# Second MLP product of a fused attention and MLP kernel by Strassen's scheme

## The chip, the cores and the metric

The kernel runs on one core of a Trainium2 chip. The metric is the device time of one execution in microseconds (us). Before the change it is 687.11 us, the median of three runs (686.88 to 687.49).

## What is computed

Softcapped attention over 4 batches, 12 heads, 448 positions and 64 columns a head, then an MLP with a squared ReLU on the 1792 tokens of 768 columns. The MLP's weights arrive in float64.

```python
scores = cap * np.tanh(scale * np.matmul(q, k.transpose(0, 1, 3, 2)) / cap)
attn = np.exp(scores - np.max(scores, axis=-1, keepdims=True))
attn = attn / (np.sum(attn, axis=-1, keepdims=True) + 1e-09)
x = np.matmul(attn, v)          # then heads side by side: 1792 x 768
h = np.maximum(x @ w_in, 0.0)   # w_in: 768 x 2048
out = h * h @ w_out             # w_out: 2048 x 768, out: 1792 x 768
```

## The kernel before

Three stretches follow each other. **Attention** runs over 24 pairs of heads. The **first product** makes `g = relu(x @ w_in)^2`, one block of 128 hidden columns (f = 0 to 15) and one batch at a time, 18 matmuls each (line 290), and writes g to DRAM (`g_dram`, line 296). The **second product** multiplies g with `w_out`. This change is about the second product.

Every float32 operand of a matmul is split in two float32r parts, a rounded one and the rest (`gh` and `gl` for g, `ohi` and `olo` for the weights), and a product takes three matmuls: high by high, high by low, low by high (lines 672 to 674). g is split by `split_g`: a DMA on SP's queue brings 1 MB of g from DRAM (line 621), ScalarE copies it to `gh` with rounding (line 624), VectorE subtracts (`gl`, line 625). The weights come by `load_wout`: a DMA of half a block of 128 rows (128x384 float64, line 258), then `decode_f64` (lines 44 to 56), which makes the two float32r parts from the 64-bit words by two ScalarE and seven VectorE instructions of 128x384. For four halves of `w_in` the last addition (line 56) is on GpSimd.

16 blocks f of weights by 14 tiles of 128 tokens by two halves `o` of 384 columns by three parts are 1344 matmuls of 384 columns. Nine of the 16 weight blocks (`NOUT1`) are decoded during the first product, seven (`wo2`) in the first part of the second. Four token tiles run side by side until all weights are there, each with its own PSUM banks; the other ten go one after the other, `gh` and `gl` in three buffers (pool `g`). `put` copies a finished 128x384 block out of PSUM on ScalarE (line 679) and writes it with two DMAs, one on SP's and one on ScalarE's queue (line 683).

Up to the end of attention the order of instructions is written by hand. Behind it a scheduler sets it by its own cost estimates, with `issue_after` holding the decoding of `w_out` behind the first product's results. Every engine, and each queue that issues DMAs, works through its list strictly in order.

Of the kernel before, what the change touches and what calls it, by code (L numbers as in the profile page):

```python
# [169 lines left out]
def tile_softcap_attention_mlp(ctx, tc, q, k, v, cap, w_in, w_out, out):  # L170
# [463 lines left out]
    marks = {NEARLY - 2: (last["square"], last["g"]), NEARLY - 1: (last["square"], last["g"])}
# [22 lines left out]

    with ExitStack() as mctx:
        op = mctx.enter_context(tc.tile_pool(name="o", bufs=2))
        gp = mctx.enter_context(tc.tile_pool(name="g", bufs=3))  # L660
        wo2 = mctx.enter_context(tc.tile_pool(name="wo2", bufs=NF - NOUT1))
        ps_o = mctx.enter_context(tc.tile_pool(name="ps_o", bufs=NSIDE - 1, space=PSUM))
        outs = {}

        def mlp2(tt, o, f):
            if f == 0 and o == 0:
                outs[tt] = (ps_o if tt % NSIDE else ps_f).tile([P, 2, 512], F32, tag="o", name="po")
            po = outs[tt]
            gh, gl = gs[tt, f]
            hi, lo = wout[f]  # L670
            os_ = slice(o * HO, (o + 1) * HO)
            nc.tensor.matmul(out=po[:, o, :HO], lhsT=gh, rhs=hi[:, os_], start=(f == 0), stop=False)  # L672
            nc.tensor.matmul(out=po[:, o, :HO], lhsT=gh, rhs=lo[:, os_], start=False, stop=False)  # L673
            nc.tensor.matmul(out=po[:, o, :HO], lhsT=gl, rhs=hi[:, os_], start=False, stop=(f == NF - 1))  # L674

        def put(tt, o):
            po = outs[tt]
# [7 lines left out]
        for f in range(FG, NF, FG):  # L685
            split_g(gp, slice(f, f + FG), side)
        for f in range(nout, NF):
            load_wout(f, wo2, scr2)
# [49 lines left out]
```

## Time and profile before

| | before |
|---|---|
| median of three runs | 687.11 us (686.88 to 687.49) |
| the profiled execution: span from first to last instruction | 684.9 us; what lies around the span is 2.2 us of the median |
| TensorE busy with matmuls | 669.2 us, 98% of the span |
| VectorE, ScalarE, GpSimd busy | 390.8, 309.7 and 113.8 us |
| second product on TensorE | 443.95 to 678.58 us of the span |

The profile is of one execution. Matmuls are pipelined, so the duration of one (335 ns for 384 columns) is longer than the distance of two starts. PE is TensorE, PEld its weight loads, DVE VectorE, ACT ScalarE, POOL GpSimd, SP the engine that issues most DMAs.

### The profile page before, as it was taken

Reading aid. Unit: us, or ns where it says so; the run is one execution under the profiler, and the core shown is the slowest. Engines: PE = TensorE matmul, PEld = TensorE weight load, DVE = VectorE, ACT = ScalarE, POOL = GpSimd, SP = SyncE. Lnnn points to the kernel's source line nnn. Section 1 sums busy time; section 2 is a strip of 40 time slices with the busy share of each in tenths; the row PEclk is TensorE's granted clock in tenths of the full one; section 3 lists DMA queues with packets and bytes.
Section 4 is the critical chain, followed back from the end, with each engine's and each line's share of the span. In section 5 each row is a group of like instructions: output and inputs, shape, how many; then the busy total and the mean of one; then the engine's idle time right before and its main releaser. Section 6 shows DMA issues by size and latency. Waiting matters only on the chain.

```text
span 684.9 us, 10575 instructions
## 1 busy us (share of the span) xinstructions
PE 669.2 (98%) x3882; PEld 549.9 (80%) x3882; DVE 390.8 (57%) x799; ACT 309.7 (45%) x454; POOL 113.8 (17%) x201
## 2 busy tenths in 40 slices
PE   6999999999999999999999999999999999999995
PEld 5444555555554799999999999999999999999995
DVE  4577878878776545599999997169840111111100
ACT  5898989878888231344334433143341111111000
POOL 8655545555420010000000000000000000000000
PEclk9999999999999999999999999999999999999999
DMA  7345446545441331475546446157544332333101
GB/s 177 86 111 137 118 120 146 133 120 121 113 113 42 118 134 68 137 226 165 182 152 201 159 157 196 66 164 211 155 108 120 85 85 84 85 85 85 34 25 28
DMA packets 95932, 83.11 MB, mean 121 GB/s; under 512 B 39072, under 2 KB 86688, under 8 KB 95872
## 3 DMA queue, kind: packets, MB, share of 16 engines
q1 hardware_dynamic: 86768, 68.50, 34.6%
q0 software_dynamic: 6112, 10.91, 6.5%
q10 hardware_dynamic: 2992, 2.93, 1.3%
q8 instruction: 33, 0.54, 0.3%
q14 instruction: 27, 0.22, 0.1%
HBM read 61.87 MB, written 20.27 MB: 120 GB/s over the span
## 4 chain that ended last, share of the span: by engine, by line
PE 96%; DMA 1%; ACT 1%; DVE 0%; SPq 0%; issue 0%; ACTq 0%; DVEq 0%
PE hps L290 34%; PE po L672 11%; PE po L673 11%; PE po L674 11%; PE sc L363 9%; PE pa L403 8%; PE pb L395 3%; PE pa L387 3%; PE tp L339 2%; PE sc L345 2%; DMA wraw<-in_moe_w_in_dram 1%; DMA kn<-in_k_dram 1%; ACT p L370 0%; SPq L321 0%; SPq L320 0%
## 5 line engine op out<-in xcount | busy, mean ns | idle before, releaser
L290 PE MATMUL hps<-xs,kqh 128*128 128x448 f32 x576 | 161.9, 362 | 0.0
L672 PE MATMUL po<-ohi,gh 128*128 128x384 f32 x448 | 149.7, 335 | 0.6 <-ACT osb L679 0.6
L673 PE MATMUL po<-olo,gh 128*128 128x384 f32 x448 | 150.0, 335 | 0.0
L674 PE MATMUL po<-ohi,gl 128*128 128x384 f32 x448 | 148.4, 335 | 0.0
L290 PEld LDWEIGHTS hps<-xs,kqh 128*128 128x128 f32 x576 | 107.9, 187 | 9.2
L290 PE MATMUL hps<-xs,kql 128*128 128x448 f32 x288 | 105.8, 367 | 0.0
L625 DVE TENSOR_TENSOR gl<-graw,gh 128x2048 fp32r<-128x2048 f32 x14 | 32.1, 2291 | 123.4 <-ACT gh L624 114.0
L370 ACT ACTIVATE p<-sc,qks 128x896 f32<-128x896 f32 x96 | 82.4, 911 | 12.7 <-PE sc L363 12.7
L375 ACT ACTIVATE p<-p,cap_sb 128x896 f32<-128x896 f32 x96 | 85.7, 948 | 0.0
L672 PEld LDWEIGHTS po<-ohi,gh 128*128 128x128 f32 x448 | 84.0, 188 | 0.9 <-ACT osb L679 0.9
L673 PEld LDWEIGHTS po<-olo,gh 128*128 128x128 f32 x448 | 84.1, 188 | 0.0
L674 PEld LDWEIGHTS po<-ohi,gl 128*128 128x128 f32 x448 | 83.9, 188 | 0.0
L294 ACT ACTIVATE r<-hps 128x448 f32<-128x448 f32 x64 | 34.7, 542 | 82.1 <-PE hps L290 78.2
L624 ACT CAST gh<-graw 128x2048 fp32r<-128x2048 f32 x14 | 26.7, 1910 | 90.6 <-PE po L673 80.8
L295 DVE TENSOR_TENSOR r<-hps,r 128x448 f32<-128x448 f32 x64 | 39.6, 620 | 47.0 <-ACT r L294 46.8
L403 PE MATMUL pa<-p,vn 128*64 128x448 f32 x288 | 59.4, 548 | 0.0
L44 ACT ACTIVATE mag<-wraw 128x384 f32<-128x384 f32 x64 | 34.7, 553 | 49.5 <-DVE olo L56 30.5
L290 PEld LDWEIGHTS hps<-xs,kql 128*128 128x128 f32 x288 | 54.1, 188 | 3.5
L290 PE MATMUL hps<-xs,whi 128*128 128x448 f32 x192 | 54.1, 363 | 0.0
L403 PEld LDWEIGHTS pa<-p,vn 128*64 128x64 f32 x288 | 18.5, 136 | 39.9 <-issue 39.9
L363 PE MATMUL sc<-kqh 64*128 64x448 f32 (+1 forms) x168 | 42.6, 441 | 5.1 <-ACT p L370 4.5
L379 DVE TENSOR_TENSOR add<-p 128x896 f32<-128x896 f32 x24 | 26.2, 1091 | 34.2 <-PE pb L395 34.2
(79 smaller groups left out, 892.0 us busy)
## 6 DMA issues: line engine op xcount, KB each, us to landing
g_dram<-r SPq DMA_DIRECT2D x64, 224.0 KB
graw<-g_dram SPq DMA_DIRECT2D x14, 1024.0 KB
wraw<-in_moe_w_in_dram SPq DMA_DIRECT2D x32, 384.0 KB
wraw<-in_moe_w_out_dram SPq DMA_DIRECT2D x32, 384.0 KB
rb<-rd SPq DMA_DIRECT2D x48, 112.0 KB
vn<-in_v_dram POOLq DMA_DIRECT2D x48, 64.0 KB, 2.7
qn<-in_q_dram SPq DMA_DIRECT2D x44, 64.0 KB
kn<-in_k_dram POOLq DMA_DIRECT2D x44, 64.0 KB, 3.1
```

Of the source, the lines that this page charges most:

```text
L44: yield nc.scalar.activation(out=magf, in_=high.bitcast(F32), func=ACTF.Abs, scale=2.0 ** 16)
L290: nc.tensor.matmul(out=ps, lhsT=w[:, c * P:(c + 1) * P], rhs=x[b, c], start=(n == 0), stop=(n == 3 * KDM - 1))
L294: nc.scalar.activation(out=r, in_=ps, func=ACTF.Relu)
L295: last["square"] = nc.vector.tensor_mul(out=r, in0=ps, in1=r)
L363: nc.tensor.matmul(out=sc[:, h, :S], lhsT=kx[r, t * P:(t + 1) * P], rhs=qx[r, 4 * P:], start=(s == 0), stop=(s == 2))
L370: nc.scalar.activation(out=p, in_=probs[n, u][:, :c, :S], func=ACTF.Tanh, scale=qks)
L375: nc.scalar.activation(out=p, in_=p, func=ACTF.Exp, scale=cap_sb)
L403: nc.tensor.matmul(out=pvs[n, 0][r], lhsT=vn[n % NKV][:, h, u - 1], rhs=p[:, h], start=False, stop=(u == NU - 1))
L625: nc.vector.tensor_sub(out=gl, in0=graw, in1=gh.bitcast(F32))
L672: nc.tensor.matmul(out=po[:, o, :HO], lhsT=gh, rhs=hi[:, os_], start=(f == 0), stop=False)
L673: nc.tensor.matmul(out=po[:, o, :HO], lhsT=gh, rhs=lo[:, os_], start=False, stop=False)
L674: nc.tensor.matmul(out=po[:, o, :HO], lhsT=gl, rhs=hi[:, os_], start=False, stop=(f == NF - 1))
```

## The change

The second product is cut into 2 by 2 blocks: tokens in two halves of seven tiles, hidden columns f in two halves of eight blocks, output columns in two halves of 384. Strassen's scheme (in Winograd's form) takes seven block products for the eight of the plain way. Each block product is seven calls of `product`, one per token tile, with 24 matmuls of 384 columns into one PSUM bank. The calls come in four stages: seven with `t11` (stage 1), seven with `t21` (stage 2), seven with `t7` (stage 3), and 28 in seven rounds with `t6`, `t5`, `t3b`, `t4b` (stage 4).

The operands are sums: four sums of weight blocks (`combine`, eight GpSimd instructions of 128x1536) and sums of tiles of g (GpSimd instructions of 128x1024, lines 762 and 774 to 776 of the new code). So the weights are first decoded to plain float32 (`decode_f32`: one ScalarE, five VectorE and one GpSimd instruction a half), summed, and then split (`split_t`, lines 655 and 656). Each tile of g is loaded as half a megabyte, summed where needed, and split by `operand` (lines 713 and 714) into one of two buffers each (`opp`). The results of the block products are added on VectorE (`put`, lines 778 and 781) and GpSimd (line 779). `raw1` holds two loaded tiles of g, `raw2` four. PSUM buffers of the first product go from five to four.

```diff
+def decode_f32(nc, pool, raw, out, n, bufs=1):
...
+    yield V.scalar_tensor_tensor(out=magf, in0=low, scalar=2.0 ** -52, in1=magf, op0=ALU.mult, op1=ALU.mult)
+    yield nc.gpsimd.tensor_add(out=out, in0=s.bitcast(F32), in1=magf)
...
-    ps_b = rctx.enter_context(tc.tile_pool(name="ps_b", bufs=5, space=PSUM))
+    ps_b = rctx.enter_context(tc.tile_pool(name="ps_b", bufs=4, space=PSUM))
...
+    ps_o = lctx.enter_context(tc.tile_pool(name="ps_o", bufs=3, space=PSUM, side="right"))
+    tw1 = lctx.enter_context(tc.tile_pool(name="tw1", bufs=10, side="right"))
+    opp = lctx.enter_context(tc.tile_pool(name="opp", bufs=2, side="right"))
+    raw1 = lctx.enter_context(tc.tile_pool(name="raw1", bufs=2, side="right"))
...
+    def split_t(src, his, los):
+        out = []
+        for g in range(2):
+            hi = his.tile([P, HG * HO], F32R, tag="t", name="th")
+            lo = los.tile([P, HG * HO], F32R, tag="t", name="tl")
+            nc.scalar.copy(out=hi, in_=src[g])
+            nc.vector.tensor_sub(out=lo, in0=src[g], in1=f32(hi))
+            out.append((hi, lo))
+        return out
+
+    def combine(op, out, x, y):
+        for g in range(2):
+            nc.gpsimd.tensor_tensor(out=out[g], in0=x[g], in1=y[g], op=op)
...
-                if nout < NOUT1:
-                    load_wout(nout, wo1, scr2)
-                    nout += 1
-                if f == NEARLY + 4:
-                    split_g(gq, slice(0, FG), side)
+                for _ in range(2):
+                    next_wout()
...
+        def operand(x):
+            hi = opp.tile([P, HF, P], F32R, tag="gh", name="gh")
+            lo = opp.tile([P, HF, P], F32R, tag="gl", name="gl")
+            nc.scalar.copy(out=hi, in_=x)
+            nc.vector.tensor_sub(out=lo, in0=x, in1=f32(hi))
+            return hi, lo
...
+        for i in range(HT):
+            s1.append(keep_s(product(operand(load_a(raw1, i, 0)), t11)))
+            for _ in range(2):
+                if quads:
+                    next_wout()
...
+        t21 = split_t(b21, tw2, tw2)
+        t1, t3, t4 = b11, b12, b21
+        combine(sub, t1, b12, b11)
+        combine(sub, t3, b22, b12)
+        t2 = raw_t(tw2)
+        combine(sub, t2, b22, t1)
+        combine(sub, t4, t2, b21)
+        t7 = split_t(t3, tw1, tw1)
+        for i in range(HT):
+            put(i, 0, s1[i], product(operand(load_a(raw1, i, 1)), t21))
+        for i in range(HT):
+            x, y = load_a(raw1, i, 0), load_a(raw2, i + HT, 0)
+            nc.gpsimd.tensor_sub(out=x, in0=x, in1=y)
+            s7.append(keep_s(product(operand(x), t7)))
+            if i == 0:
+                t6 = split_t(t2, tw2, tw2)
+            if i == 2:
+                t5 = split_t(t1, tw2, tw2)
+            if i == 4:
+                t3b = split_t(b22, tw1, tw1)
+        t4b = split_t(t4, tw2, tw1)
+        for i in range(HT):
+            r21, r22 = load_a(raw2, i + HT, 0), load_a(raw2, i + HT, 1)
+            r11, r12 = load_a(raw1, i, 0), load_a(raw2, i, 1)
+            nc.gpsimd.tensor_add(out=r21, in0=r21, in1=r22)
+            nc.gpsimd.tensor_sub(out=r11, in0=r21, in1=r11)
+            nc.gpsimd.tensor_sub(out=r12, in0=r12, in1=r11)
+            po = product(operand(r11), t6)
+            nc.vector.tensor_add(out=s1[i], in0=s1[i], in1=po)
+            nc.gpsimd.tensor_add(out=s7[i], in0=s7[i], in1=s1[i])
+            po = product(operand(r21), t5)
+            nc.vector.tensor_add(out=s1[i], in0=s1[i], in1=po)
+            put(i + HT, 1, s7[i], po)
+            put(i, 1, s1[i], product(operand(r12), t3b))
+            put(i + HT, 0, s7[i], product(operand(r22), t4b), sub)
```

Where this puts work in the engines' lists is seen at three places. First GpSimd, around the beginning of the second product. Before, its last work was four additions for `w_in`, and then the load of a flag that ends the kernel:

```order
L310 DMA vn3_114<-in_v_dram 64x256
L56 TENSOR_TENSOR kql_2803<-t_2807,mag_2806 128x384
L56 TENSOR_TENSOR kql_2803<-t_2872,mag_2871 128x384
L56 TENSOR_TENSOR kql_2930<-t_2934,mag_2933 128x384
L56 TENSOR_TENSOR kql_2930<-t_2992,mag_2991 128x384
L615 TENSOR_LOAD far_87
```

Now the additions of the decoding (L75) stand there with the sums of weight blocks between them (L662, `tr` is a half of a block of weights) and the sums of g behind them (L762, `a` is a loaded tile of g):

```order
L75 TENSOR_TENSOR tr_4987<-s_5062,mag_5060 128x384
L662 TENSOR_TENSOR tr_4558<-tr_4987,tr_4558 128x1536
L75 TENSOR_TENSOR tr_4988<-s_5107,mag_5105 128x384
L662 TENSOR_TENSOR tr_5229<-tr_4987,tr_3210 128x1536
L662 TENSOR_TENSOR tr_3212<-tr_5229,tr_3212 128x1536
L75 TENSOR_TENSOR tr_4988<-s_5119,mag_5117 128x384
L75 TENSOR_TENSOR tr_4988<-s_5164,mag_5162 128x384
L75 TENSOR_TENSOR tr_4988<-s_5176,mag_5174 128x384
L662 TENSOR_TENSOR tr_4559<-tr_4988,tr_4559 128x1536
L662 TENSOR_TENSOR tr_5230<-tr_4988,tr_3211 128x1536
L662 TENSOR_TENSOR tr_3213<-tr_5230,tr_3213 128x1536
L762 TENSOR_TENSOR a_5488<-a_5488,a_5490 128x1024
```

So six of the eight block sums, and all 28 sums of g, came into a stretch in which GpSimd had nothing to do.

Second VectorE, where the last weights are decoded and split. Before, the decoding of one half stood around each subtraction for g:

```order
L45 TENSOR_SCALAR mag<-mag 128x384
L54 SCALAR_TENSOR_TENSOR mag<-wraw,mag 128x384
L55 TENSOR_TENSOR t<-s,ohi 128x384
L48 TENSOR_SCALAR t<-mag 128x384
L56 TENSOR_TENSOR olo<-t,mag 128x384
L50 SCALAR_TENSOR_TENSOR s<-wraw,t 128x384
L625 TENSOR_TENSOR gl<-graw,gh 128x2048
```

Now, at the beginning of stage 2, the subtractions that split the weight sums (L656) stand between those for g (L714) and the additions of results (L730):

```order
L714 TENSOR_TENSOR gl_5246<-a_5243,gh_5245 128x1024
L656 TENSOR_TENSOR tl_5236<-tr_4558,th_5235 128x1536
L656 TENSOR_TENSOR tl_5525<-tr_5229,th_5524 128x1536
L714 TENSOR_TENSOR gl_5281<-a_5278,gh_5280 128x1024
L656 TENSOR_TENSOR tl_5240<-tr_4559,th_5239 128x1536
L730 TENSOR_TENSOR osb_5274<-s_4871,po_5249 128x384
L656 TENSOR_TENSOR tl_5685<-tr_4987,th_5684 128x1536
L714 TENSOR_TENSOR gl_5316<-a_5313,gh_5315 128x1024
L656 TENSOR_TENSOR tl_5529<-tr_5230,th_5528 128x1536
L730 TENSOR_TENSOR osb_5309<-s_4928,po_5284 128x384
L714 TENSOR_TENSOR gl_5351<-a_5348,gh_5350 128x1024
```

The subtraction that TensorE waits for came behind others of 128x1536, which wait for GpSimd's sums.

Third SP's queue late in the second product. Before, one load of g for each tile of tokens, and two outputs:

```order
L621 DMA graw_6062<-g_dram_82 128x16x128
L683 DMA out_0_dram<-osb_5784 64x384
L683 DMA out_0_dram<-osb_5836 64x384
L621 DMA graw_6173<-g_dram_82 128x16x128
L683 DMA out_0_dram<-osb_5895 64x384
```

Now one round of stage 4 (`a_6198`, `a_6200`, `a_6202`, `a_6204` are the four tiles of round 3; loads of two rounds stand among the outputs of an earlier one):

```order
L707 DMA a_6202<-g_dram_82 128x8x128
L734 DMA out_0_dram<-osb_5910 64x384
L707 DMA a_6058<-g_dram_82 128x8x128
L707 DMA a_6062<-g_dram_82 128x8x128
L734 DMA out_0_dram<-osb_5986 64x384
L707 DMA a_6198<-g_dram_82 128x8x128
L734 DMA out_0_dram<-osb_6019 64x384
L707 DMA a_6344<-g_dram_82 128x8x128
L734 DMA out_0_dram<-osb_6052 64x384
L707 DMA a_6200<-g_dram_82 128x8x128
L707 DMA a_6204<-g_dram_82 128x8x128
```

Four loads of half the size took the place of one, with three outputs between them that wait for results.

## Rows read from the trace of the kernel before

**Rows 1.** The page: busy time, share of the span and instructions of each engine.

```profile
PE 669.2 (98%) x3882; PEld 549.9 (80%) x3882; DVE 390.8 (57%) x799; ACT 309.7 (45%) x454; POOL 113.8 (17%) x201
```

**Rows 2.** The page: the chain that ended last, by engine and by line.

```profile
PE 96%; DMA 1%; ACT 1%; DVE 0%; SPq 0%; issue 0%; ACTq 0%; DVEq 0%
PE hps L290 34%; PE po L672 11%; PE po L673 11%; PE po L674 11%; PE sc L363 9%; PE pa L403 8%; PE pb L395 3%; PE pa L387 3%; PE tp L339 2%; PE sc L345 2%; DMA wraw<-in_moe_w_in_dram 1%; DMA kn<-in_k_dram 1%; ACT p L370 0%; SPq L321 0%; SPq L320 0%
```

**Rows 3.** Busy time in stretches (columns in the first line): first product, second product's two parts.

```profile
core 0: us, PE busy (x) PEld busy (x) DVE busy (x) ACT busy (x) POOL busy (x), PEclk, DMA share, GB/s
300.00:420.00 120.00, 120.00 (x595) 111.25 (x594) 110.61 (x262) 50.26 (x100) 0.00 (x0) 1.00 0.56 181
...
447.00:502.00 55.00, 55.00 (x317) 55.00 (x316) 45.05 (x91) 22.04 (x31) 0.00 (x0) 1.00 0.52 159
502.00:678.00 176.00, 175.43 (x1011) 175.11 (x1010) 19.77 (x11) 27.27 (x35) 0.00 (x0) 1.00 0.28 79
```

**Rows 4.** Timeline, TensorE: start, duration; the second product's first matmuls and its last.

```profile
443.95 0.33 PE L672 MATMUL po<-ohi,gh 128*128 128x384 f32 x1
444.12 0.34 PE L673 MATMUL po<-olo,gh 128*128 128x384 f32 x1
...
678.24 0.34 PE L674 MATMUL po<-ohi,gl 128*128 128x384 f32 x1
```

**Rows 5.** Timeline: the end of the program behind the last matmul.

```profile
678.61 0.48 ACT L679 COPY osb<-po 128x384 f32<-128x384 f32 x1 [8.80 <-PE po L674]
679.11 0.47 SPq L683 DMA_DIRECT2D out_dram<-osb  x1
```

**Rows 6.** Groups of instructions, shapes apart: count, busy us, mean ns; 446 to 686 us.

```profile
L672 PE MATMUL po<-ohi,gh 128*128 128x384 f32 x448 | 149.7, 335 | 0.6 <-ACT osb L679 0.6
L624 ACT CAST gh<-graw 128x2048 fp32r<-128x2048 f32 x13 | 24.8, 1910 | 90.3 <-PE po L673 80.8 <-DMA graw<-g_dram 9.5
L52 ACT CAST ohi<-s 128x384 fp32r<-128x384 f32 x14 | 7.0, 510 | 3.8 <-DVE s L50 3.8
```

**Rows 7.** Groups of VectorE's instructions, shapes apart, whole program.

```profile
L295 DVE TENSOR_TENSOR r<-hps,r 128x448 f32<-128x448 f32 x64 | 39.6, 620 | 47.0 <-ACT r L294 46.8
L54 DVE SCALAR_TENSOR_TENSOR mag<-wraw,mag 128x384 f32<-128x384 uint32 x64 | 34.5, 550 | 0.2
L50 DVE SCALAR_TENSOR_TENSOR s<-wraw,t 128x384 uint32<-128x384 uint32 x64 | 34.5, 552 | 0.4
L625 DVE TENSOR_TENSOR gl<-graw,gh 128x2048 fp32r<-128x2048 f32 x14 | 32.1, 2291 | 123.4 <-ACT gh L624 114.0 <-DMA out_dram<-osb 9.4
L379 DVE TENSOR_TENSOR add<-p 128x896 f32<-128x896 f32 x24 | 26.2, 1091 | 34.2 <-PE pb L395 34.2
L45 DVE TENSOR_SCALAR mag<-mag 128x384 f32<-128x384 f32 x64 | 22.5, 354 | 8.7 <-ACT mag L44 8.5
```

**Rows 8.** Groups of GpSimd's instructions, shapes apart, whole program.

```profile
L56 POOL TENSOR_TENSOR kql<-t,mag 128x384 fp32r<-128x384 f32 x4 | 4.1, 1025 | 74.9 <-DVE t L55 74.9
L720 POOL MEMSET const-bfloat16-1.0<- 128x1 bf16 x1 | 0.1, 102 | 0.0
```

**Rows 9.** Timeline, GpSimd's first two additions and what VectorE ran beside them.

```profile
237.74 1.02 POOL L56 TENSOR_TENSOR kql<-t,mag 128x384 fp32r<-128x384 f32 x1 [40.83 <-DVE t L55]
246.09 1.06 POOL L56 TENSOR_TENSOR kql<-t,mag 128x384 fp32r<-128x384 f32 x1 [7.34 <-DVE t L55]
...
237.61 0.62 DVE L295 TENSOR_TENSOR r<-hps,r 128x448 f32<-128x448 f32 x1
...
245.93 0.35 DVE L45 TENSOR_SCALAR mag<-mag 128x384 f32<-128x384 f32 x1
```

**Rows 10.** One load of 1 MB of g: its issue, then stretches of 1 us (last column GB/s).

```profile
552.50 0.36 SPq L621 DMA_DIRECT2D graw<-g_dram  x1
...
554.00:555.00 1.00, 1.00 (x8) 1.00 (x7) 0.00 (x0) 0.00 (x0) 0.00 (x0) 1.00 0.87 230
555.00:556.00 1.00, 1.00 (x7) 1.00 (x7) 0.00 (x0) 0.00 (x0) 0.00 (x0) 1.00 1.07 324
556.00:557.00 1.00, 1.00 (x8) 1.00 (x7) 0.00 (x0) 0.00 (x0) 0.00 (x0) 1.00 1.16 315
557.00:558.00 1.00, 1.00 (x8) 1.00 (x7) 0.00 (x0) 0.00 (x0) 0.00 (x0) 1.00 1.00 289
558.00:559.00 1.00, 1.00 (x8) 1.00 (x7) 0.00 (x0) 0.00 (x0) 0.00 (x0) 1.00 0.04 14
```

More of the change, by code (lines that the diff above doesn't have):

```diff
@@ L631, in tile_softcap_attention_mlp, with raw_t, load_wout @@
-    side = slice(0, NSIDE * P)
-    nout = 0
+    f32 = lambda t: t.bitcast(F32)
+    HG = HF // 2
+    def raw_t(pool):
+        return [pool.tile([P, HG * HO], F32, tag="t", name="tr") for _ in range(2)]
+    def load_wout(dst, f, o):
+        raw = fetch_w(scr2, f, o * HO, False, 3)
+        g, c = divmod(f % HF, HG)
+        for _ in decode_f32(nc, scr2, raw, dst[g][:, c * HO:(c + 1) * HO], HO, 2):
+            pass
+    def split_t(src, his, los):
[7 more added lines that the diff above has]
+        return out
@@ L633, in tile_softcap_attention_mlp @@
+    marks = {NEARLY - 2: (last["square"], last["g"]), NEARLY - 1: (last["square"], last["g"])}
     BEHIND = 3
[L634 removed]
     for f in range(NEARLY, NF):
@@ L652, in tile_softcap_attention_mlp @@
         marks[f] = last["square"], last["g"]
-    while nout < NOUT1:
-        load_wout(nout, wo1, scr2)
-        nout += 1
     rctx.close()
     with ExitStack() as mctx:
[L659 to L677, printed above, removed]
-            osb = op.tile([P, HO], F32, tag="osb", name="osb")
-            nc.scalar.copy(out=osb, in_=po[:, o, :HO])
@@ new lines, in operand, with product @@
+        def operand(x):
[4 more added lines that the diff above has]
+            return hi, lo
+        def product(x, t):
+            xh_, xl_ = x
+            po = ps_o.tile([P, 512], F32, tag="o", name="po")[:, :HO]
+            for c in range(HF):
+                th, tl = t[c // HG]
+                cols = slice(c % HG * HO, (c % HG + 1) * HO)
+                for i, (w, m) in enumerate(((xh_, th), (xh_, tl), (xl_, th))):
+                    nc.tensor.matmul(out=po, lhsT=w[:, c], rhs=m[:, cols], start=(c == 0 and i == 0),
+                                     stop=(c == HF - 1 and i == 2))
+            return po
@@ L680, in put @@
+        def put(tt, o, x, y, op=ALU.add):
+            osb = ob.tile([P, HO], F32, tag="osb", name="osb")
+            nc.vector.tensor_tensor(out=osb, in0=x, in1=y, op=op)
             for a in range(2):
@@ L683, in put @@
                 (nc.scalar if a else nc.sync).dma_start(out=dst, in_=osb[a * D:(a + 1) * D])
[L685 to L688, printed above, removed]
-        for first in range(0, NF, FG):
-            for tt in range(NSIDE):
-                for f in range(first, first + FG):
-                    for o in range(2):
-                        mlp2(tt, o, f)
-                if first + FG == NF:
-                    for o in range(2):
-                        put(tt, o)
@@ L697, in tile_softcap_attention_mlp, with keep_s @@
-        for tt in range(NSIDE, NT // P):
-            split_g(gp, slice(0, NF), slice(tt * P, (tt + 1) * P))
-            for o in range(2):
-                for f in range(NF):
-                    mlp2(tt, o, f)
-                put(tt, o)
+        def keep_s(po):
+            s = sv.tile([P, HO], F32, tag="s", name="s")
+            nc.scalar.copy(out=s, in_=po)
+            return s
+        add, sub = ALU.add, ALU.subtract
+        s1, s7 = [], []
+        for i in range(HT):
[3 more added lines that the diff above has]
+                    next_wout()
@@ new lines, in tile_softcap_attention_mlp @@
+        while quads:
+            next_wout()
+        t21 = split_t(b21, tw2, tw2)
[18 more added lines that the diff above has]
+                t3b = split_t(b22, tw1, tw1)
```

53 lines of the change are left out of this document (37 added, 16 removed).

## The prediction

> **What bounds the kernel now.** The busy times first: TensorE is busy 98% of the span, VectorE 57%, ScalarE 45%, GpSimd 17% [rows 1]. The chain of waits says the same of the end: 96% of it is TensorE, and a third (lines 672 to 674, 11% each) is the second product [rows 2]. In the stretches of the second product TensorE is busy 55.0 of 55.0 us and 175.4 of 176.0, at a granted clock of 1.00 (its 2.4 GHz level), while GpSimd does nothing; VectorE has 45.1 us of work in the first 55 us and 19.8 in the other 176 [rows 3]. So a matmul less is worth its full distance as long as its operands come in time. From the first start at 443.95 us to the last at 678.24 there are 1343 distances: 0.1744 us each [rows 4]. Behind the last matmul come one copy and the output's DMAs [rows 5]; the same follows in the new code, with VectorE's addition in the copy's place, so the end (684.9 - 678.6 = 6.3 us) stays. The sum is made against 687.1, the median, which is the profiled execution's 684.9 us span and 2.2 us around it.
>
> **What goes.** Seven products for eight leave 49 calls of 24 matmuls, 1176 for 1344. 168 x 0.1744 = **29.3 us** less on TensorE; shapes, weight loads and columns are the same, so the distance is taken as unchanged. Without any wait the time would be 687.1 - 29.3 = 657.8. A product now lasts 24 x 0.1744 = 4.19 us, stages 1 and 2 together 58.7 us, stage 3 29.3, stage 4 117.2.
>
> **What comes, by engine.** ScalarE's rounding copy took 510 ns for 384 columns and 1910 for 2048 [rows 6]: 0.841 ns a column between them, so 1.05 us for a tile of g (1024), 1.48 for 1536. VectorE's addition or subtraction out of SBUF took 1091 ns for 896 columns and 2291 for 2048 [rows 7]: 1.042 a column, so 1.22 us for `gl`, 1.76 for a weight sum's `tl`; a half's decoding on VectorE is now 3 x 0.35 + 2 x 0.55 = 2.15 us (lines 45, 50, 54 stand for the new ones), where it was 3.25. GpSimd's addition of 128x384 took 1.025 us [rows 8]. Its 1024 and 1536 are not in the trace: in proportion 2.73 and 4.10 us; with the 0.1 us of its smallest instruction as a fixed part, 2.58 and 3.82. I take 2.73 and 4.10, the upper ones, since only that row is its own kind. The Trainium skill (GPSIMD Engine Reference, Elementwise, side-by-side cycle accounting) has 4497 ns for 2048 columns of such an addition; between that and the row an estimate is 2.36 and 3.43 us, and GpSimd's load in stages 1 and 2 below would be 28.8 us for 32.8, which makes the forecast 2 us shorter.
>
> **What lies beside TensorE.** A product needs `gh` at its first matmul and `gl` at its third. `opp` has two buffers, so a split can begin only when the product before the last has ended, that is, when the product ahead starts. Copy 1.05, subtraction 1.22 and some 0.2 of hand-over are 2.5 us in a window of 4.19 + 0.35 = 4.5: **2.0 us to spare** a product, and none can be saved up. That cover hides all splitting; what takes VectorE longer than 2.0 us out of turn stands on the path.
> In the first product VectorE is busy 110.6 of 120 us and TensorE never waits [rows 3]. There the decoding changes from 18 halves of 3.25 us to 20 of 2.15 (15.5 us less) with one split of weights more (3.5): nothing on the path. One PSUM buffer less leaves three products (11 us) of lead. Price if that cover is gone: below, under the second rival.
>
> **The unknown: VectorE and GpSimd at once.** The trace has GpSimd's additions beside VectorE for moments only: one beside a multiplication with an input in PSUM (both at their usual 1.02 and 0.62 us), one beside the last 0.19 us of a 128x384 instruction (1.06 us) [rows 9]. Neither shows two instructions that each read two SBUF tiles. So the price of their meeting is bounded: at the one end nothing, at the other each GpSimd instruction keeps VectorE from starting for its whole length.
> - Stages 1 and 2, 58.7 us: GpSimd has 8 x 1.03 + 6 x 4.10 = 32.8 us. VectorE has 14 `gl` (17.1), 9 `tl` (15.8), 6 halves (12.9) and 7 additions of results (0.55 each from line 295's 620 ns for 448 columns, 3.9): 49.7 us, so 9.0 us are free. If GpSimd holds VectorE up for half of its time, 16.4 - 9.0 = **7.4 us** come onto the path; for all of it, 23.8.
> - Stage 3, 29.3 us: GpSimd 7 x 2.73 = 19.1, VectorE 7 x 1.22 + 3 x 1.76 = 13.9, 15.4 free: 0 at half, 3.7 at full. Besides, a loop through `raw1`'s two buffers: load, sum, copy, subtract, load again. A load of 1 MB issued at 552.50 has landed by 558.0, its data from 554 on at up to 324 GB/s [rows 10]: half of it some 1.5 + 2.0 = 3.5 us. 3.5 + 2.73 + 1.05 + 1.22 + 0.5 = 9.0 us for two products of 8.4: 0.3 a product, 2 in all, which the 2.0 to spare just covers; with some waits 2 us show. I take **2**; at full 6.
> - Stage 4, seven rounds of 16.8 us. In a round, counted from the start of its second product: the addition of line 779 ends at 1.7, the load `r22` of the next round (free to go when this round's `r21` is split, 1.6 before) has landed at 2.2, the two sums end at 4.9 and 7.7, copy and subtraction at 8.8 and 10.1, and they are needed at 12.6 and 12.9: 2.8 us to spare. One at a time, the sums fall between the splits (sums 3.0 to 5.8 and 7.0 to 9.8), the third sum (9.8 to 12.5) stands ahead of the subtraction, and that ends at 13.7: 0.8 late, 6 us in seven rounds. I take half, **3**. Four loads and three outputs a round (2.7 MB in 16.8 us, 160 GB/s) are half of the rate seen.
>
> Half is taken because an instruction that comes at any moment of another one waits for half of it on average. 7.4 + 2 + 3 = 12.4, and the forecast is 657.8 + 12.4 = **670.2 us**.
>
> **Rivals.**
> 1. *They hardly meet, and all splitting is hidden.* For it: the additions of rows 9 kept their length beside VectorE. Against: neither row has the case. 657.8, and up to 663 with the loads' 2 and a few late splits. Chance 0.28.
> 2. *Slower: one at a time.* Place: stages 1 and 2, where GpSimd's block sums of 4.10 us follow each other and the `gl` that TensorE waits for stands on VectorE's list behind `tl`s and decoding. Price: 23.8 + 6 + 6 = 35.8, time 693.6; with the first product, where 22 additions and two block sums (31 us) then meet a VectorE with some 9 + 12 us free, up to 9 more. It outweighs the gain from the point where GpSimd's time keeps VectorE waiting for over 86% of its length (12.4 at 50%, 35.8 at 100%, the gain is 29.3). For it: both lists are in order, so one late instruction holds all behind it. Against: where VectorE waits for TensorE anyway, GpSimd's sums pass for free. Chance 0.21. The Trainium skill (SBUF, State Buffer, section Who interferes with whom) says it as a rule: "A DVE instruction with two SBUF inputs contends with a GpSimd instruction that reads SBUF", and the second to issue is blocked until the first is done. No row here shows it; by it the time is this rival's 693.6.
> 3. *The loads are late.* Stage 3 asks for some 13 half megabytes in 29.3 us, 232 GB/s of the 324 seen. At 5.5 us a load, what 1 MB took, the loop is 11.0 us for two products, 1.3 a product: 9 less 2 to spare, 7 us. 664.8 without other waits, 677 with the forecast's. Chance 0.06.
> 4. *Near no change*, 685.7 to 688.5: the way from the forecast to the second rival leads through it. Chance 0.07.
> That the new code doesn't do what it says is not open: its list on TensorE has 1176 of these matmuls.
>
> **How the numbers follow.** Forecast 670.2 (664 to 685), chance 0.38. Faster by over 0.2% (what a measurement of this kernel can tell from no change, 1.4 us) are the forecast, the first and the third rival: 0.72. Same 0.07, slower 0.21. The range reaches from the first rival's 658 to 695, just past the second's price: what is left out is some 0.05 below and 0.1 above.
>
> **What would show it.** Right: 1176 matmuls with 0.174 us between starts, the second product some 217 us long from its first matmul, TensorE's idle time put down to `gl` of line 714, most of it in stages 1 and 2, and VectorE's subtractions starting late or running long just where a GpSimd sum of 4 us runs. First rival: TensorE without idle time, the second product 206 us. Second: VectorE's starts line up with GpSimd's ends, stage after stage. Third: ScalarE's copy of line 713 or GpSimd's line 762 waits for the load of line 707. Wrong altogether: GpSimd's 1024 or 1536 columns far from 2.73 and 4.10 us, a granted clock that falls in the waits, or a first product that ends later than at 444 us.

## The result, and the profile after

The changed kernel takes 693.88 us (median of 4, 692.81 to 694.88) where the one before took 687.23 beside it: the ratio is 1.0096 [1.0081, 1.0110], so it is slower by 1%. (In brackets stands the 95% interval; the ratios below too are to the kernel before, run beside each.) The forecast was 670.2 us and faster; the second rival, 693.6 us and slower, gave the time almost to the digit, though not by its own sum, as shown below.

The busy line of the changed kernel's page (busy us, share of the span, instructions), which answers to [rows 1]:

```profile
PE 650.6 (94%) x3714; PEld 527.3 (76%) x3714; DVE 498.2 (72%) x826; ACT 334.1 (48%) x457; POOL 271.1 (39%) x276
```

and the chain that ended last, by engine and then by line, which answers to [rows 2]:

```profile
PE 72%; DVE 11%; DMA 5%; issue 4%; POOL 3%; ACT 2%; SPq 1%; POOLq 0%; DVEq 0%; ACTq 0%
```

TensorE's busy share fell from 98% to 94%, and its share of the chain from 96% to 72%; VectorE (11%, `gl` of line 714 alone 4%), the loads of `a` (4%) and GpSimd (3%) came in. GpSimd works 39% of the span where it was 17%, VectorE 72% where it was 57%.

The second product stage by stage, beside [rows 3]. Columns: length of the stretch, then busy time and instructions of TensorE, its weight loads, VectorE, ScalarE and GpSimd, then granted clock, DMA share and GB/s:

```profile
446.00:510.00 64.00, 46.28 (x225) 44.70 (x225) 57.78 (x51) 25.92 (x30) 35.92 (x13) 0.81 0.52 149
510.00:527.00 17.00, 17.00 (x100) 17.00 (x100) 8.37 (x9) 5.70 (x5) 4.31 (x2) 1.00 0.62 178
527.00:562.00 35.00, 30.40 (x164) 29.45 (x164) 16.91 (x10) 13.56 (x15) 22.78 (x9) 0.95 0.72 204
562.00:684.00 122.00, 119.30 (x679) 117.24 (x677) 71.98 (x65) 29.51 (x30) 58.09 (x26) 1.00 0.45 128
```

Reading: a matmul is worth 0.1744 us, so 225 of them are 39.2 us of work in the first 64 us: **24.8 us lost**. TensorE stood for 17.7 us, and the 46.3 us in which it worked were 7.0 longer than the work, at a mean clock of 0.81. The next 17 us, to the end of stage 2, lose nothing (100 matmuls). Stage 3 (527 to 562) loses 35 - 164 x 0.1744 = 6.4 us, stage 4 (to the last matmul's end at 683.3) 2.9. Together some 34 us, where the change takes 29.3 away. The first product ends as before (first matmul of the second at 443.5 us). Behind the last matmul,

```profile
682.95 0.33 PE L724 MATMUL po<-th,gl 128*128 128x384 f32 x1
```

lie 7.7 us to the end of the span at 691.0, where it was 6.3 before: another 1.4 us.

Where TensorE stood: VectorE's instructions (start, length, engine, line, operation, shapes), GpSimd's, and TensorE's that began after an idle time (in brackets, with what it waited for):

```profile
454.94 3.58 DVE L73 TENSOR_SCALAR mag<-s 128x384 uint32<-128x384 uint32 x1
...
459.03 1.22 DVE L714 TENSOR_TENSOR gl<-a,gh 128x1024 fp32r<-128x1024 f32 x1
...
462.65 3.64 DVE L68 TENSOR_SCALAR mag<-mag 128x384 f32<-128x384 f32 x1
466.21 5.06 DVE L656 TENSOR_TENSOR tl<-tr,th 128x1536 fp32r<-128x1536 f32 x1
...
486.05 8.94 DVE L656 TENSOR_TENSOR tl<-tr,th 128x1536 fp32r<-128x1536 f32 x2 [1.02 <-ACT th L655]
494.91 4.50 DVE L714 TENSOR_TENSOR gl<-a,gh 128x1024 fp32r<-128x1024 f32 x1
```

```profile
454.56 3.74 POOL L662 TENSOR_TENSOR tr<-tr 128x1536 f32<-128x1536 f32 x1
...
461.08 8.58 POOL L662 TENSOR_TENSOR tr<-tr 128x1536 f32<-128x1536 f32 x2
...
484.02 14.31 POOL L662 TENSOR_TENSOR tr<-tr 128x1536 f32<-128x1536 f32 x3
```

```profile
460.30 0.69 PE L724 MATMUL po<-th,gl 128*128 128x384 f32 x1 [3.46 <-DVE gl L714]
...
472.73 0.69 PE L724 MATMUL po<-th,gl 128*128 128x384 f32 x1 [5.38 <-DVE gl L714]
...
499.47 0.69 PE L724 MATMUL po<-th,gl 128*128 128x384 f32 x1 [8.21 <-DVE gl L714]
```

A GpSimd block sum starts at 454.56 and ends at 458.30; the VectorE operation of line 73 that starts at 454.94 lasts 3.58 us and ends at 458.52, although alone it takes 0.36. `gl` can only follow it, at 459.03, and TensorE stands 3.46 us. The same at 462.65 (line 68, 3.64 us) and 466.21 (`tl`, 5.06 for 1.75), with 5.38 us for TensorE, and at 484 to 498, where three sums in a row stretch two `tl` to 8.94 us and `gl` to 4.50, with 8.21 us. Here GpSimd and VectorE work one at a time.

The clock: stretches of 5 us beside the same waits, columns as above.

```profile
456.00:461.00 5.00, 1.54 (x7) 1.22 (x6) 4.96 (x4) 0.77 (x2) 4.11 (x2) 0.82 1.13 312
461.00:466.00 5.00, 5.00 (x17) 5.00 (x17) 5.00 (x2) 3.09 (x4) 5.00 (x2) 0.50 1.13 333
466.00:471.00 5.00, 1.35 (x8) 1.03 (x6) 5.00 (x2) 1.53 (x2) 3.58 (x2) 0.84 0.15 36
471.00:476.00 5.00, 3.27 (x10) 3.27 (x11) 5.00 (x11) 0.00 (x0) 1.03 (x1) 0.50 0.36 105
```

After each standstill the granted clock is 0.50 (the 1.2 GHz level, 17 matmuls in 5 us where 29 fit at 2.4 GHz) for several us of work. In [rows 3] it was 1.00 throughout, with no standstill.

### The profile page after: what moved, and what is told of

It reads as the page before. It is cut to its first block, busy times and chain, and to the rows that moved or that the text cites. A ratio compares the mean times of both kernels' runs of the same rounds, so it can differ in the third digit from the quotient of the medians.

```text
span 691.0 us, 10567 instructions
## 1 busy us (share of the span) xinstructions
PE 650.6 (94%) x3714; PEld 527.3 (76%) x3714; DVE 498.2 (72%) x826; ACT 334.1 (48%) x457; POOL 271.1 (39%) x276
## 4 chain that ended last, share of the span: by engine, by line
PE 72%; DVE 11%; DMA 5%; issue 4%; POOL 3%; ACT 2%; SPq 1%; POOLq 0%; DVEq 0%; ACTq 0%
PE hps L309 29%; PE po L724 16%; PE sc L382 9%; PE pa L422 8%; DVE gl L714 4%; DMA a<-g_dram 4%; PE pb L414 3%; PE pa L406 3%; PE tp L358 2%; PE sc L364 2%; POOL a L775 1%; DVE tl L656 1%; DVE t L70 1%; ACT gh L713 1%; DVE mag L73 1%
## 5 line engine op out<-in xcount | busy, mean ns | idle before, releaser
L724 PE MATMUL po<-th,gl 128*128 128x384 f32 x392 | 136.2, 348 | 23.6 <-DVE gl L714 23.5
L724 PE MATMUL po<-th,gh 128*128 128x384 f32 x392 | 134.6, 343 | 0.7 <-ACT gh L713 0.7
L724 PE MATMUL po<-tl,gh 128*128 128x384 f32 x392 | 134.4, 343 | 0.0
L713 ACT CAST gh<-a 128x1024 fp32r<-128x1024 f32 x49 | 51.6, 1052 | 135.4 <-PE po L724 77.1
L714 DVE TENSOR_TENSOR gl<-a,gh 128x1024 fp32r<-128x1024 f32 x49 | 84.4, 1722 | 35.8 <-ACT gh L713 35.8
L75 POOL TENSOR_TENSOR tr<-s,mag 128x384 f32<-128x384 f32 x32 | 38.3, 1199 | 150.7 <-DVE mag L74 135.9
L724 PEld LDWEIGHTS po<-th,gl 128*128 128x128 f32 x392 | 76.2, 194 | 27.6 <-DVE gl L714 27.6
L724 PEld LDWEIGHTS po<-th,gh 128*128 128x128 f32 x392 | 76.1, 194 | 1.0 <-ACT gh L713 1.0
L724 PEld LDWEIGHTS po<-tl,gh 128*128 128x128 f32 x392 | 76.0, 194 | 0.0
L328 POOL DMA_DIRECT2D vn<-in_v_dram x48 | 26.0, 541 | 82.0 <-PE pa L422 82.0
L398 DVE TENSOR_TENSOR add<-p 128x896 f32<-128x896 f32 x24 | 26.2, 1092 | 34.1 <-PE pb L414 34.1
```

Of the source, the lines that this page charges most:

```text
L75: yield nc.gpsimd.tensor_add(out=out, in0=s.bitcast(F32), in1=magf)
L398: nc.vector.tensor_add(out=adds[n], in0=probs[n, 1], in1=probs[n, 2])
L713: nc.scalar.copy(out=hi, in_=x)
L714: nc.vector.tensor_sub(out=lo, in0=x, in1=f32(hi))
L724: nc.tensor.matmul(out=po, lhsT=w[:, c], rhs=m[:, cols], start=(c == 0 and i == 0), stop=(c == HF - 1 and i == 2))
```

## The experiments

Theory A: while a GpSimd instruction reads SBUF (the memory on the chip that holds the tiles), VectorE's instructions with two inputs in SBUF don't run, and by the expectation of e1 those in a fast mode neither; no row names the mode of an instruction. The Trainium skill has the case of two inputs as a rule (SBUF — State Buffer, Who interferes with whom). The runs below agree with it: `tl`, with two inputs, took 3.13 us on average beside the sums and 1.75 without them. Theory B: the holds don't matter; GpSimd's sums are long, and splits and products wait for them in the order of the lists. Theory C: buffers and loads are late.

**Left out, piece by piece.** e1 is without the block sums (`combine` isn't called, and `t2 = b22`), e3 without the sums of `g` too; the cut shows e1's edit:

```diff
-        combine(sub, t1, b12, b11)
-        combine(sub, t3, b22, b12)
-        t2 = raw_t(tw2)
-        combine(sub, t2, b22, t1)
-        combine(sub, t4, t2, b21)
+        t2 = b22
```

e1, block sums out:

> The eight sums of weight blocks on GpSimd (128x1536) are left out, so the products take unsummed weights; everything else stays. Theory A (a VectorE instruction that reads two SBUF tiles, or runs in its fast mode, does not run while GpSimd reads SBUF): stages 1 and 2 lose their idle time (17.1 us in 446 to 505 us and 3.6 in the 30 us behind) and the low clock that follows it, 668 to 674 us. Rival B (TensorE waits for the sums themselves, which come late by the order of the lists): the same here; what tells them apart is the next kernel.

Measured 677.05 us, 0.9851 [0.9835, 0.9868]: 16.8 us less than the changed kernel, and 3 us over the 668 to 674 that theory A gave. Then e3, both out:

> The sums of weight blocks and the 28 sums of tiles of g are left out; GpSimd keeps the last addition of the decoding and seven additions of results. Theory A: nearly all of the gain of 29.3 us shows: second product 206 to 210 us, 658 to 663 us. Rival C (the loads of g and the two operand buffers hold the products up, whatever GpSimd does): 668 us or more, with waits for loads of line 707.

Measured 666.85 us, 0.9704 [0.9688, 0.9720]: above theory A's 663, below C's 668, so neither's. And e8, with the block sums kept and the sums of `g` out:

```diff
-            x, y = load_a(raw1, i, 0), load_a(raw2, i + HT, 0)
-            nc.gpsimd.tensor_sub(out=x, in0=x, in1=y)
+            x = load_a(raw1, i, 0)
...
-            nc.gpsimd.tensor_add(out=r21, in0=r21, in1=r22)
-            nc.gpsimd.tensor_sub(out=r11, in0=r21, in1=r11)
-            nc.gpsimd.tensor_sub(out=r12, in0=r12, in1=r11)
```

> The sums of g (lines 762 and 774 to 776) are left out, with the second of the two loads that line 762 needs; the block sums stay on GpSimd. Theory A: the g sums hold gl up in stages 3 and 4 as the block sums do in stages 1 and 2, and the two costs add: 693.9 - (677.05 - 666.85) = 683.7, that is 681 to 687. Rival E (what is lost in stages 3 and 4 is only the tail of what the block sums delayed): 690 to 694.

Measured 684.34 us, 0.9961 [0.9949, 0.9973], as theory A's sum had it. The costs add: the block sums are worth 693.88 - 677.05 = 16.8 or 684.34 - 666.85 = 17.5, the sums of `g` 10.2 or 9.5, and 666.85 - 657.8 = 9.0 us are lost with no sum in the program. That last part is new. In e3's trace 6.8 of them lie at 446 to 510 us (64 us with 328 matmuls); the rest is some 1.4 us at either end, where the second product's first matmul comes at 445.4 and 7.7 us lie behind the last one, as in the changed kernel. The part at 446 to 510, in e3's stretches:

```profile
456.00:461.00 5.00, 5.00 (x31) 5.00 (x30) 4.00 (x4) 2.50 (x4) 1.93 (x1) 1.00 1.13 311
461.00:466.00 5.00, 1.82 (x9) 1.18 (x8) 5.00 (x5) 3.49 (x5) 0.00 (x0) 0.99 0.68 217
466.00:471.00 5.00, 3.68 (x11) 3.68 (x12) 4.48 (x9) 1.42 (x2) 1.25 (x1) 0.50 0.60 169
471.00:476.00 5.00, 5.00 (x26) 5.00 (x26) 3.08 (x5) 1.62 (x3) 1.05 (x1) 0.83 0.14 41
510.00:540.00 30.00, 30.00 (x175) 30.00 (x174) 14.95 (x12) 14.52 (x17) 0.00 (x0) 1.00 0.46 131
```

From 461 to 471 us, in stage 1, TensorE stands 4.5 us, runs at 0.50 and comes back in the next 5; later stretches, as the last row, are full at 1.00. TensorE's two waits, and ScalarE's list in that place (brackets: idle time and what ended it):

```profile
463.72 0.45 PE L724 MATMUL po<-th,gh 128*128 128x384 f32 x1 [1.52 <-ACT gh L713]
...
467.32 0.69 PE L724 MATMUL po<-th,gh 128*128 128x384 f32 x1 [2.98 <-ACT gh L713]
```

```profile
459.04 0.56 ACT L67 ACTIVATE mag<-wraw 128x384 f32<-128x384 f32 x1 [2.50 <-DMA wraw<-in_moe_w_out_dram]
459.50 1.47 ACT L655 CAST th<-tr 128x1536 fp32r<-128x1536 f32 x1
...
461.24 1.49 ACT L655 CAST th<-tr 128x1536 fp32r<-128x1536 f32 x1
462.62 1.05 ACT L713 CAST gh<-a 128x1024 fp32r<-128x1024 f32 x1
...
466.22 1.05 ACT L713 CAST gh<-a 128x1024 fp32r<-128x1024 f32 x1 [1.72 <-DMA a<-g_dram]
```

The rounding of a raw weight (line 67) waits 2.50 us for its load; behind it on the list stand the `th` copies for stage 2, and behind these the `gh` for which TensorE waits 1.52 us. The next `gh`, for which it waits 2.98, is late by its own load of `a` (1.72 us). DMA moves 311 GB/s just before (see the windows above, 456:461).

**What in a block sum costs.** e2: the sum replaced by a fill of its output; e9: by three fills, as long as a sum:

```diff
-            nc.gpsimd.tensor_tensor(out=out[g], in0=x[g], in1=y[g], op=op)
+            for _ in range(3):
+                nc.gpsimd.memset(out[g], 0.5)
```

> The eight sums of weight blocks become GpSimd instructions of the same size on the same tiles that only write (a fill with 0.5): same place in the lists, same waits, no reading of SBUF; the values are not the sums. Theory A: VectorE's 128x384 and 128x1536 instructions keep their usual 0.35 and 1.75 us beside the fills, 668 to 676 us. Rival B: what waits for GpSimd still waits, less only by what a fill is shorter than a sum: over 680 us, and VectorE's long instructions stay where the fills are.

Measured 674.83 us, 0.9827 [0.9811, 0.9843]: in theory A's range, under B's. It is also 2.2 us under e1, which has no instruction there at all: an edit moves other work in the lists too, so a difference of 2 us between two of these kernels isn't the sums' alone.

> Each block sum of line 662 is replaced by three fills of its output with a constant, one behind the other on GpSimd (the sums themselves are left out). One fill took 1.42 us, so GpSimd is busy 3 x 1.42 = 4.25 us for each, as long as the sum's 4.1 us, and the splits behind wait for it as they wait for the sum; but a fill reads nothing. Theory A (GpSimd's reads of SBUF hold VectorE up): as with one fill, 674.8, up to 678, and VectorE's decode steps beside the fills take 0.35 us. Theory B (the length of GpSimd's sums in the order of the lists costs the time, whatever they read): near the changed kernel, 688 to 695.

Measured 680.17 us, 0.9893 [0.9876, 0.9909]: between the two, nearer A. For about the same GpSimd time (34.1 us in 24 fills, 33.5 in eight sums) the fills cost 3.1 us more than no block sums at all, the sums 16.8: some four fifths of the price, 13.7 us, go with the reads (of the 19.1 us over e2, seven tenths). The rest can be the order of the lists (theory B) or holds by the fills themselves; the runs don't separate them. The fills also stand in somewhat other places than the sums, since they don't wait for the halves that a sum reads; for those the sums hardly waited (GpSimd's idle time before line 662 at 446 to 510 us is 0.3 us, see below). The trace of e9 shows both a hold and none. GpSimd, then VectorE beside it:

```profile
468.39 5.91 POOL L663 MEMSET tr<- 128x1536 f32 x4 [2.87 <-DVE tl L656]
```

```profile
469.25 1.23 DVE L715 TENSOR_TENSOR gl<-a,gh 128x1024 fp32r<-128x1024 f32 x1 [0.65 <-ACT gh L714]
470.40 1.06 DVE L68 TENSOR_SCALAR mag<-mag 128x384 f32<-128x384 f32 x1
471.38 0.54 DVE L72 SCALAR_TENSOR_TENSOR s<-wraw,t 128x384 uint32<-128x384 uint32 x1
471.84 1.14 DVE L70 TENSOR_SCALAR t<-mag 128x384 uint32<-128x384 uint32 x1
472.90 1.62 DVE L73 TENSOR_SCALAR mag<-s 128x384 uint32<-128x384 uint32 x1
```

While four fills run from 468.39 to 474.30, `gl` (two inputs) keeps its 1.23 us and line 72 (two inputs too) its 0.54, but the one-input operations of lines 68, 70 and 73, 0.35 us alone, take 1.06, 1.14 and 1.62. So theory A held for the two-input operations, and what its expectation said of the decode steps beside fills did not.

e4: each block sum in four GpSimd instructions of a quarter (128x384), the same work in the same place:

> Each block sum on GpSimd in four instructions of 128x384. GpSimd's reading time stays the same (some 33 us or a little more), but none lasts longer than 1.1 us. Theory A: VectorE's instructions there last at most some 1.1 us longer each instead of 3.5 to 4; TensorE's idle time in stages 1 and 2 falls by a third to two thirds, 678 to 688 us. Rival B: no change or longer by GpSimd's extra instructions, 692 to 697 us.

Measured 686.38 us, 0.9990 [0.9980, 1.0000]: 7.5 us less than in one piece, at 1.45 us a quarter (5.8 us a sum, more GpSimd time than the 3.7 to 4.8 of one piece). That is in theory A's range. Theory B, by which more time should cost more, is out for that part. At 446 to 510 us (the stretch, then `tl`):

```profile
446.00:510.00 64.00, 51.58 (x272) 49.60 (x271) 59.08 (x52) 28.68 (x32) 45.20 (x31) 0.95 0.55 158
```

```profile
L656 DVE TENSOR_TENSOR tl<-tr,th 128x1536 fp32r<-128x1536 f32 x7 | 14.3, 2040 | 2.6 <-ACT th L655 2.4
```

Worked out as for the changed kernel below, VectorE's instructions are stretched by 21 us in all here too, but a `tl` takes 2.04 us and not 3.13, TensorE stands 12.4 us and not 17.7, and its mean clock is 0.95: what counts is how long one hold lasts.

**The sums on VectorE.** e5 moves the block sums (line 662), e6 the sums of `g` too, e7 writes e6's block sums behind the products of stage 2:

```diff
-            nc.gpsimd.tensor_tensor(out=out[g], in0=x[g], in1=y[g], op=op)
+            nc.vector.tensor_tensor(out=out[g], in0=x[g], in1=y[g], op=op)
```

> The eight block sums of line 662 are issued to VectorE, all else as in the changed kernel. Theory A (GpSimd's reads of SBUF hold VectorE up): the eight sums cost VectorE 8 x 1.76 us = 14.1 us by the uncontended tl subtractions of the same shape, in place of 33.5 us of GpSimd in which VectorE stood; the decode steps and splits at 446 to 510 us go back to 0.35 and 1.76 us. The time is that without block sums, 677.05, plus 0 to 10 us for the 14.1 us ahead of gl: 677 to 687. Theory C (operand loads are what is late in stages 1 and 2): the time hardly moves, 690 to 695.

Measured 682.61 us, 0.9943 [0.9923, 0.9962], inside theory A's range and well under C's 690. VectorE's groups at 446 to 510 us in e5 (busy us, mean ns, idle before):

```profile
L656 DVE TENSOR_TENSOR tl<-tr,th 128x1536 fp32r<-128x1536 f32 x7 | 12.2, 1753 | 0.6 <-ACT th L655 0.6
...
L662 DVE TENSOR_TENSOR tr<-tr 128x1536 f32<-128x1536 f32 x6 | 10.4, 1754 | 0.9 <-POOL tr L75 0.9
...
L73 DVE TENSOR_SCALAR mag<-s 128x384 uint32<-128x384 uint32 x6 | 2.1, 357 | 0.1
L68 DVE TENSOR_SCALAR mag<-mag 128x384 f32<-128x384 f32 x5 | 1.8, 354 | 2.0 <-ACT mag L67 2.0
```

and the same groups in the changed kernel:

```profile
L662 POOL TENSOR_TENSOR tr<-tr 128x1536 f32<-128x1536 f32 x6 | 26.5, 4419 | 0.3
L656 DVE TENSOR_TENSOR tl<-tr,th 128x1536 fp32r<-128x1536 f32 x7 | 21.8, 3126 | 1.0 <-ACT th L655 1.0
...
L714 DVE TENSOR_TENSOR gl<-a,gh 128x1024 fp32r<-128x1024 f32 x9 | 15.3, 1704 | 2.5 <-ACT gh L713 2.5
...
L68 DVE TENSOR_SCALAR mag<-mag 128x384 f32<-128x384 f32 x6 | 5.4, 898 | 0.0
L73 DVE TENSOR_SCALAR mag<-s 128x384 uint32<-128x384 uint32 x6 | 5.3, 890 | 0.1
```

With the block sums' reads gone from GpSimd, `tl` is back from 3126 to 1753 ns, line 73 from 890 to 357, line 68 from 898 to 354, and the sum itself takes 1.75 us on VectorE for 4.4 on GpSimd.

> The block sums and the 32 sums of g (lines 762 and 774 to 776) are issued to VectorE; GpSimd keeps the additions of the decoder and of line 779 (128 x 384). Theory A: a sum of g costs VectorE 1.23 us (gl's shape) in place of a GpSimd instruction of 2.5 to 3.0 us that stretches gl from 1.23 to 1.72 us; a stage-4 quarter of four products (16.7 us of TensorE) then holds 4 x 1.23 + 3 x 1.23 + 4 x 0.55 = 10.8 us of VectorE, so nothing waits there: 667 to 678, at least 6 us under the run with block sums alone moved. Rival D (VectorE becomes the bound, since its list is in order): no better than that run, 680 or more.

Measured 681.75 us, 0.9928 [0.9907, 0.9949]: a miss for theory A and as rival D had it, 0.9 us better than e5, within the intervals. Moving the sums of `g` (28, not the 32 of the expectation) gained nothing that can be told. In the trace the sums, 1.23 us each, stand ahead of `gl` on VectorE's own list; that this eats the gain is not shown.

> As the run with all sums on VectorE, and the eight block sums are written one behind each product of stage 2 (the pair t1, then t3, t2, t4), with the split of t3 behind the fourth. Theory A with a bunching of VectorE's list as the remaining cause: the 14.1 us of block sums fit into the 4.18 - 1.78 = 2.4 us that VectorE has free in each of the eight products of stage 2: 662 to 672, 2 to 8 us under the run before it. Rival D (VectorE's total in stages 1 to 3 is the bound wherever the sums stand): within 2 us of it.

Measured 682.29 us, 0.9931 [0.9904, 0.9958], no change. (A stage has seven products, so the eighth sum, the second half of `t4`, is left out in this run.) It doesn't test the place: in its trace the first two sums run at 425.86 and 439.88, in the first product, and three more by 473, in stage 1, so the program's scheduler had drawn them ahead. So e10 holds them, with the splits of `t7`, `t6` and `t5`, behind the operand of a product (`behind()` opens `tc.issue_after` for its `gh` and `gl`), and lets the loads of stages 1 and 2 alternate between two pools:

```diff
+            if i == 1:
+                with behind():
+                    combine(sub, t1, b12, b11)
...
+            x = operand(load_a((raw1, raw2)[i % 3 > 0], i, 1))
```

> All sums on VectorE as in the run with all of them moved (681.75), but the block sums and the splits of t7, t6 and t5 are held behind the operand of a chosen product on both lists (ScalarE and VectorE), where 14 of them had been drawn ahead of gl, and the loads of the operands of stages 1 and 2 alternate between the pools raw1 and raw2, so that six stand ahead and not two. Theory F (what is left over 666.85, the run without sums, is the place of the sums and splits in lists kept in order, and the loads that wait for buffers): 669 to 676. Rival D (VectorE's total in stages 1 to 3 is the bound, 56 us of 70 there): 679 to 684.

Measured 676.75 us, 0.9836 [0.9812, 0.9860]: 0.75 us over theory F's range and 2.25 under D's. The pinning and the alternating loads weren't run apart. It computes all that the kernel before does and beats both, by 10.9 us and 17.1 us; of the 29.3 us that the seven products save it keeps 10.9. The 9.9 us over e3, which has neither sums nor pinning, are about what the sums still cost on VectorE. TensorE's waits for `gl` (us in total, times, longest), in e10 and in the changed kernel:

```profile
PE po L731 <- DVE gl L713: 8.6, 5, 3.4
```

```profile
PE po L724 <- DVE gl L714: 23.5, 8, 8.2
```

**The nine microseconds without sums.** e11 and e12 decode three halves of the weights a step in the first product and one a product in stage 1 (e11 without sums, e12 on e10); e13 and e14 issue the loads of stage 1's operands from GpSimd's queue and not from SP's:

```diff
-                for _ in range(2):
-                    next_wout()
+                for _ in range(3):
+                    if len(quads) > HF:
+                        next_wout()
```

```diff
-            s1.append(keep_s(product(operand(load_a(raw1, i, 0)), t11)))
+            s1.append(keep_s(product(operand(load_a(raw1, i, 0, nc.gpsimd)), t11)))
```

> The block sums and the sums of g are left out, as in the run of 666.85, and three halves of the second weights are decoded a step of the first product in place of two, until eight are left; stage 1 then decodes one half a product, not two. Theory G (the 9 us that the run without sums lies over 657.8 are the decoder's loads and steps at 456 to 470 us, which stand ahead of gh and gl on the lists): 658 to 663. Rival H (they belong to the change of the products, buffers or loads of g themselves): 665 to 669.

> All sums on VectorE and pinned, as in the run of 676.75, with the same earlier decoding. Theory G: 5 to 9 us less, 668 to 672. Rival H: 675 to 678.

> The block sums and the sums of g are left out, as in the run of 666.85, and the loads of stage 1's operands (line 707 there) are issued from GpSimd's queue and not from SP's, where they stand behind the last stores of g and the loads of the weights. Theory J (the 9 us over 657.8 come from the order of SP's list: the loads wait there behind stores that wait for the first product's end, then come in a burst at 310 GB/s in which the weights' loads and with them ScalarE's list are late): 658 to 664. Rival K (stage 1 asks for more than the DMA engines give, 0.52 + 2 x 0.39 MB in 4.18 us, 313 GB/s, in whichever order): 665 to 669.

> All sums on VectorE and pinned, as in the run of 676.75, with the loads of stage 1's operands issued from GpSimd's queue. Theory J: 668 to 673. Rival K: 675 to 679.

Measured 665.88 us (0.9683 [0.9664, 0.9703]) and 679.03 us (0.9868 [0.9840, 0.9896]) for the earlier decoding, 664.78 us (0.9672 [0.9656, 0.9688]) and 679.50 us (0.9897 [0.9878, 0.9916]) for the queue: 1 to 2 us less without sums, 2 to 3 more with them, and but for the last these lie within the intervals. Neither theory G nor J gets its gain. In e13 the same stretch stands as in e3:

```profile
456.00:461.00 5.00, 5.00 (x31) 5.00 (x30) 4.42 (x4) 2.57 (x3) 2.77 (x2) 1.00 1.08 317
...
466.00:471.00 5.00, 3.42 (x11) 3.42 (x12) 4.52 (x8) 1.16 (x2) 2.13 (x2) 0.51 0.44 116
```

DMA moves 311 and 317 GB/s at 456 to 461 in whichever order, nearly the 324 at the peak of [rows 10] (333 in the changed kernel at 461 to 466), and then TensorE stands, at a clock that falls to 0.51. That fits the amount of the loads (rival K), but no run took a load of stage 1 away, and e2 speaks against the amount alone. It has the same loads in stage 1, but other places in the lists:

```profile
456.00:461.00 5.00, 5.00 (x31) 4.88 (x29) 4.75 (x3) 2.30 (x3) 5.00 (x4) 1.00 1.10 311
461.00:466.00 5.00, 2.45 (x13) 1.92 (x12) 5.00 (x7) 3.82 (x5) 1.57 (x2) 1.00 0.52 153
466.00:471.00 5.00, 5.00 (x31) 4.91 (x30) 5.00 (x8) 3.85 (x5) 1.06 (x1) 1.00 0.53 149
```

At the same rate before, TensorE stands 2.55 us here and not 4.5, and its clock stays at 1.00; one `th` copy, not two, stands on ScalarE's list between the late raw weight and `gh`. So the order of the lists has a part in it. How the 9 us divide stays open; what is shown is that they are lost with no sum in the program, and cured by neither the one queue nor the earlier decoding.

## Why the prediction was wrong

- **TensorE's saving** (29.3 us) was right: 1176 matmuls, and where nothing waits (e3 from 476 us on) they follow at the old distance.
- **The step that failed is the sum for stages 1 and 2, "7.4 us come onto the path"**, from which the direction came. Measured are 24.8 us (the first row of the windows above), in three parts. (1) *The share.* "GpSimd holds VectorE up for half of its time": by the groups above, `tl` was stretched by 7 x 1.37 us, `gl` by 9 x 0.48, lines 68 and 73 by 6 x 0.54 and 6 x 0.53, lines 72 and 74 by 0.7 each; together 21.9 us of 35.9 in which GpSimd worked, 61%. Less the 9.0 that were free this is 12.9 for the prediction's 7.4, and TensorE indeed stood 17.7 - 4.5 = 13.2 us more than in e3. An instruction waits half of another's length on average when it comes at any moment; but behind a held instruction the next one comes at once, when the next GpSimd sum has just begun, as at 484 to 498 us. (That this makes the whole difference from half is not shown.) (2) *The clock*: 7.0 us, 2.3 of them in e3 too (328 matmuls there in 59.5 us of the same 64). The prediction named a granted clock that falls in the waits as what would make it wrong, and put no price on it. (3) *What is lost without sums*: idle 4.5 and clock 2.3. The prediction's list had every VectorE instruction of the stages, but in no order, and no wait for a load in stage 1 at all. Together 12.9 + (7.0 - 2.3) + (4.5 + 2.3) = 24.4 us.
- **Stages 3 and 4** were taken at 2 + 3 = 5 us; the trace shows 6.4 + 2.9, the runs 9.5 to 10.2 for the sums of `g`. Stage 4 came out at half as put, stage 3 at its full end (6).
- **The end** behind the last matmul was taken to stay at 6.3 us; it is 7.7.
- **The second rival** named the mechanism, its place and the engine, and the verdict. Its price, 35.8 us, came out (34 in the trace), but not by its full hold: GpSimd kept VectorE for 61% of its time in stages 1 and 2, not over 86%, and the clock and the loads, which it had not priced, made up the difference. That its time was met is luck.
- **The third rival** (loads late) was looked for in stage 3. Its sign is there (line 762 waits 10.1 us for loads of line 707 at 527 to 562 us), but TensorE's longest wait in stage 3, 2.98 us, ends with a `gl` that took 2.92 us beside such a sum. In stage 1 of e3, where the decoder's loads come on top of those of `g`, late loads do reach TensorE.
- **GpSimd's durations**: 4.10 and 2.73 us were assumed. The first block sum above took 3.74 and, one behind the other, 4.3 to 4.8; a sum of `g` took 2.40 alone and 2.5 to 3.2 on average by line. That guess was good.

## What to carry to other kernels

Work put on GpSimd beside a VectorE whose list is in order and on the path is not free: price it by the stretch of VectorE's instructions, not by GpSimd's idle time, and give it in short pieces if it must be there: here nearly the same total stretch, in quarters, cost 7.5 us less. When TensorE is the bound and has one product of lead, add to every standstill the slow matmuls behind it. If helper work goes onto the engine that splits the operands, hold it behind the operand of a given product; a scheduler that draws it ahead as soon as its inputs are there spends the lead. Here that, with more loads ahead, was worth 5.0 us (e6 to e10).

## What the runs showed of the hardware

- A two-input VectorE subtraction of 128x1536 takes 1.75 us alone and up to 5.06 beside GpSimd's additions; a one-input operation of 128x384 goes from 0.35 to 3.64. An addition with one input in PSUM (line 730) kept its 0.55 us in the changed kernel in all 28 cases, as at 531.23 beside a GpSimd sum that ran from 530.01 to 533.53.
- GpSimd's fills (1.42 us for 128x1536) left two-input operations alone and stretched one-input ones from 0.35 to 1.06 to 1.62 us. That was not expected.
- GpSimd's additions are stretched too: 128x384 from 1.02 us [rows 8] to a mean of 1.36 in stage 1 of the changed kernel (line 75, seven of them in 9.5 us at 446 to 484).
- After standstills of 3.5 to 8 us TensorE's granted clock was 0.50 (1.2 GHz); behind the 3.46 us that ended at 460.30 it was 0.50 for the whole of 461 to 466. In e3 it was 0.50 behind a wait of 2.98 us too; in e2 it stayed at 1.00 behind waits of 1.71 and 0.84.
